# An order of 2,178 steps drawn anew, and a planner that lets each engine go on by itself: attention, SwiGLU and SoLU layers on one core

## The chip, the core and the metric

The kernel runs on one core of a Trainium2 chip. The metric is the device time of one execution in microseconds, as the median of several runs; less is better. The engines are named as in the profile: PE (TensorE, matmuls), DVE (VectorE), ACT (ScalarE), POOL (GpSimd) and SP (SyncE, which issues the DMAs).

## What is computed

```python
def _attn_ref(q, k, v):                      # q, k, v: (4, 8, 576, 64), float32
    scores = scale * np.matmul(q, k.transpose(0, 1, 3, 2))
    # heads 0-3: the last 32 keys; heads 4-7: every fourth of the last 128
    scores = np.where(masks[None], scores, -1000000000.0)
    scores = scores - np.max(scores, axis=-1, keepdims=True)
    attn = np.exp(scores)
    attn = attn / (np.sum(attn, axis=-1, keepdims=True) + 1e-09)
    return np.matmul(attn, v)
def _moe_ref(x, w_gate, w_val, w_out):       # x: (2304, 512), d_ff 1536
    g = x @ w_gate
    silu = g * (1.0 / (1.0 + np.exp(-g)))
    return silu * (x @ w_val) @ w_out
def _moe2_ref(x, w_in, w_out, g_ln):         # d_ff 1024
    h = x @ w_in
    e = np.exp(h - np.max(h, axis=-1, keepdims=True))
    solu = h * (e / (np.sum(e, axis=-1, keepdims=True) + 1e-09))
    # layer norm over d_ff, times g_ln
    return ln @ w_out
```

The weights are float64 in memory; each is turned into two float16 halves (a high part and the rest) on the chip, and so are the activations, so that three float16 products make one product of nearly float32's precision.

## The kernel before

**The work.** Attention is done by batch (4), pair of heads (4) and group of three blocks of 96 queries (2): 32 groups. A group runs scores on PE (line 1208), the maximum on DVE (L1230), exponentials with their sums on ACT (L1249), the inverse of the six sums per row on DVE (`inv`: L1262 adds 1e-9 and scales, L1264 is the reciprocal), the product with it on POOL (L1268), transposes on PE (L1293) and a copy of them to SBUF (L1301 on DVE, L1304 on ACT), the product with V (L1331), and the split of the output into two halves, on ACT (L600) and DVE (L605). Line 605 is a helper that writes the low half of any split, so tiles tell the uses apart: `x` is an attention output, `yhl` the output of the first MoE layer, `uhl` its hidden values, `area` and `gv` weights.

The 2,304 rows then go through the MoE layer in 12 chunks of 192 (`a_chunk`, six parts each, L1395: gate and value; `b_part`, L1479: the product with `w_out`), and through the second layer in 18 tiles of 128 (`c_part`, L1527; `d_part`, L1655). Thirteen slabs of weights are loaded by L669 in halves, converted on DVE, ACT and POOL (L685 to L741), given a scale common to the slab (L768, L793, L794 and a sum over partitions by PE, L544), and split. `w_rel`, called three times, makes the scales of several slabs relative to the largest of them: L894 to L896, and L901 in the second call.

**What sets the order.** Every piece of work is a *step*: an engine, a cost in microseconds, a function that issues its instructions, and the tiles it reads and writes. 2,178 steps are recorded; the table `PRI` gives each its place in one total order. `Plan.schedule` goes through that order once, with a model of times. The model decides two things: which PSUM bank a step gets, and how many *fillers* are put ahead of a PE step that has to wait. A filler is a matmul of ones (`idle`, L376) that nobody reads; it keeps PE active while it waits, and is issued only in the plan's first 320 us (`OPT["fill"]`). Each engine's queue is then the order restricted to that engine, and the queues run on the chip as their semaphores allow: a step whose inputs are late holds up what stands behind it on its engine.

In the model of before a step starts when its engine is free, its inputs are there and, for steps marked `port`, when no step of the other engine of DVE and POOL that is planned already overlaps it.

Of the kernel before, what the change touches and what calls it, by code (L numbers as in the profile page):

```python
# [1942 lines left out]
```

## Time and profile before

| | before |
|---|---|
| median of 3 runs | 753.19 us (752.01 to 753.53) |
| profiled execution | 754.8 us |
| its span, first to last instruction | 751.7 us |
| mean granted clock of PE | 0.986 of full speed |
| PE busy | 727.3 us (97%) |
| DVE busy | 503.2 us (67%) |
| ACT busy | 448.1 us (60%) |
| POOL busy | 236.5 us (31%) |
| fillers | 225, busy 31.4 us |

The shares are means over very different stretches. Up to about 200 us attention, the conversion of weights and the first chunks run side by side; from 280 us PE is busy without a gap. The busy time of PE holds the fillers, and matmuls that ran at the lower of PE's two clocks (the granted clock is the profile's column PEclk, 1.00 being full speed).

### The profile page before, as it was taken

The numbers are of one execution on the slowest core, as the hardware profiler recorded it, in microseconds if no ns is written. First come the engines' busy times: TensorE is split into PE (matmuls) and PEld (weight loads), VectorE is DVE, ScalarE is ACT, GpSimd is POOL, SyncE is SP. The second block draws the span as 40 slices with busy tenths as digits, with TensorE's granted clock in tenths as the row PEclk, the third lists the DMA queues.
The fourth block names the chain that finished last, engine by engine and source line by source line (L and its number), as shares of the span: only waits on it lengthen the run. The fifth ranks groups of instructions, "written<-read, shape, count | busy, mean of one in ns | idle before, by whom it ended". The sixth has DMA issues, their size and how long they took to land.

```text
span 751.7 us, 18305 instructions
## 1 busy us (share of the span) xinstructions
PE 727.3 (97%) x7488; PEld 601.0 (80%) x7488; DVE 503.2 (67%) x1059; ACT 448.1 (60%) x982; POOL 236.5 (31%) x188
## 2 busy tenths in 40 slices
PE   9868999999899999999999999999999999999998
PEld 7747989998897896678775989998776889968744
DVE  4989989899867877786787755366568222134562
ACT  5878997757566585976764664466554333334432
POOL 4525354865552331161252233314131000100000
PEclk9979999999999999999999999999999999999999
DMA  9797744236153614647455244213522100001021
GB/s 222 177 371 214 206 129 150 77 103 165 37 150 104 118 26 85 117 94 150 89 111 114 67 68 106 57 41 62 97 58 59 36 9 15 2 1 30 15 35 50
DMA packets 150195, 71.71 MB, mean 95 GB/s; under 512 B 136416, under 2 KB 136416, under 8 KB 149600
## 3 DMA queue, kind: packets, MB, share of 16 engines
q1 hardware_dynamic: 150112, 70.55, 39.0%
q8 instruction: 58, 0.95, 0.5%
q14 instruction: 25, 0.20, 0.1%
HBM read 46.14 MB, written 4.72 MB: 68 GB/s over the span
## 4 chain that ended last, share of the span: by engine, by line
PE 72%; DVE 7%; ACT 2%; issue 1%; POOL 0%; ACTq 0%; DVEq 0%; POOLq 0%
PE ps L1395 28%; PE ps L1479 16%; PE ps L1655 12%; PE ps L1527 12%; PE ps L1208 2%; PE ps L1336 1%; DVE area L715 1%; DVE uhl L605 1%; DVE uhl L596 0%; DVE wam L692 0%; PE ps L1331 0%; DVE sml L1230 0%; DVE area L605 0%; PE ps L1636 0%; DVE area L1561 0%
## 5 line engine op out<-in xcount | busy, mean ns | idle before, releaser
L1395 PE MATMUL ps<-x,gv 128*128 128x192 f16 x3456 | 296.1, 247 | 1.8 <-ACT ps L577 0.6
L1395 PEld LDWEIGHTS <-gv 128*128 128x128 f16 x3456 | 286.5, 98 | 7.3 <-issue 2.4
L1479 PE MATMUL ps<-uhl,area 128*128 128x192 f16 x1728 | 152.6, 247 | 1.6 <-DVE yhl L605 1.3
L1479 PEld LDWEIGHTS <-area 128*128 128x128 f16 x1728 | 143.7, 98 | 7.1 <-DVE yhl L605 1.5
L1527 PE MATMUL ps<-area,yhl 128*128 128x512 f16 x432 | 98.7, 379 | 0.0
L1655 PE MATMUL ps<-area 128*128 128x512 f16 x408 | 94.0, 379 | 0.0
L1268 POOL TENSOR_TENSOR sm<-sm,sml 96x768 f32<-96x768 f32 x28 | 45.5, 1627 | 126.3 <-DVE sml L1264 69.5
L1416 DVE SCALAR_TENSOR_TENSOR u<-ps,c_gv,si 128x384 f32<-128x384 f32 x60 | 36.5, 611 | 62.8 <-ACT si L1407 56.3
L1527 PEld LDWEIGHTS <-yhl 128*128 128x128 f16 x432 | 41.1, 98 | 46.0
L1407 ACT ACTIVATE si<-ps,c_gv 128x384 f32<-128x384 f32 x72 | 41.3, 578 | 53.6 <-PE ps L1395 49.1
L1655 PEld LDWEIGHTS <-area 128*128 128x128 f16 x408 | 38.8, 98 | 41.9 <-issue 0.2
L617 POOL TENSOR_TENSOR uhl<-u,uhl 128x768 f16<-128x768 f32 x12 | 20.1, 1686 | 92.3 <-ACT uhl L600 92.2
L685 POOL TENSOR_TENSOR area<-area 128x512 int32<-128x512 int32 x28 | 38.5, 1392 | 33.3 <-ACT area L698 11.0
L1587 POOL TENSOR_TENSOR sml<-sml,nhalf 128x2 f32<-128x2 f32 x18 | 12.9, 720 | 113.9 <-DVE sml L1584 113.9
L617 POOL TENSOR_TENSOR qk<-qk,qk 96x768 f16<-96x768 f32 x16 | 27.8, 1737 | 66.7 <-ACT qk L600 29.5
L1422 ACT ACTIVATE si<-u 128x384 f32<-128x384 f32 x60 | 31.0, 517 | 21.5 <-DVE u L1416 21.4
L1249 ACT ACTIVATE sm<-sm,sml 96x128 f32<-96x128 f32 x96 | 37.2, 388 | 6.1 <-DVE sml L1243 6.0
L1546 DVE TENSOR_REDUCE sml<-ps 128x1 f32<-128x1024 f32 x18 | 21.9, 1214 | 21.8 <-PE ps L1527 21.8
L1552 ACT ACTIVATE area<-ps,sml 128x1024 f32<-128x1024 f32 x18 | 21.7, 1203 | 22.1 <-DVE sml L1547 21.6
L605 DVE SCALAR_TENSOR_TENSOR area<-area,rel 128x512 f16<-128x512 f32 x30 | 26.2, 880 | 10.8 <-ACT area L600 10.7
L376 PE MATMUL ps<-ones 128*128 128x256 bf16 x225 | 31.4, 291 | 1.0 <-POOL ones L1681 1.0
L1607 ACT ACTIVATE area<-area,sml 128x1024 f32<-128x1024 f32 x17 | 20.9, 1238 | 18.5 <-DVE sml L1601 18.5
(226 smaller groups left out, 1131.0 us busy)
## 6 DMA issues: line engine op xcount, KB each, us to landing
area<-in_moe_w_out_dram SPq DMA_DIRECT2D x10, 1024.0 KB, 5.1
area<-in_moe_w_val_dram SPq DMA_DIRECT2D x6, 1024.0 KB, 7.7
area<-in_moe_w_gate_dram SPq DMA_DIRECT2D x6, 1024.0 KB, 9.9
out_dram<-area SPq DMA_DIRECT2D x18, 256.0 KB, 2.1
area<-in_moe_w_in_dram SPq DMA_DIRECT2D x4, 1024.0 KB, 5.1
qk<-in_v_dram SPq DMA_DIRECT2D x9, 384.0 KB, 4.0
v<-in_v_dram SPq DMA_DIRECT2D x49, 64.0 KB, 2.3
qk<-in_q_dram SPq DMA_DIRECT2D x20, 144.0 KB, 5.5
```

The source lines that it names most:

```text
L376: nc.tensor.matmul(out=to, lhsT=ones, rhs=ones.unsqueeze(1).to_broadcast([128, 2, 128]), start=True, stop=True)
L605: step("DVE", dve(n) + by + more, lambda: nc.vector.scalar_tensor_tensor(out=lo(), in0=src(), scalar=scale, in1=hi(), op0=ALU.mult, op1=AL ...
L617: step("POOL", n / 480 + 0.05, lambda: nc.gpsimd.tensor_tensor(out=lo(), in0=src(), in1=hi(), op=ALU.subtract), r=list(sk) + list(hk), w=lk)
L685: step("POOL", 1.23, lambda: nc.gpsimd.tensor_tensor(out=ti[:, x], in0=ti[:, x], in1=part[:, x], op=ALU.add), r=rk, w=tk)
L1249: nc.scalar.activation(out=smv[:, n], in_=view()[0:QB, n // 3, n % 3] if on_pe else smv[:, n], func=ACTF.Exp, bias=nm[:, n:n + 1], scale=c ...
L1268: step("DVE" if OPT["pn"][b] else "POOL", dve(768) if OPT["pn"][b] else 1.43, lambda: on.tensor_tensor(out=smv, in0=smv, in1=rs.unsqueeze( ...
L1395: nc.tensor.matmul(out=view()[:, ff, w], lhsT=wt[:, a, kk, (f % 4) * 128:(f % 4) * 128 + 128], rhs=x[:, c, kk, BLK * o:BLK * o + BLK], sta ...
L1407: step("ACT", act(384) + 0.06, lambda: nc.scalar.activation(out=si, in_=view()[:, :, 0], func=ACTF.Silu, scale=c_gv[:, b, 2 * ci:2 * ci + 1]),
L1416: nc.vector.scalar_tensor_tensor(out=uu, in0=view()[:, :, 1], scalar=c_gv[:, b, 2 * ci + 1:2 * ci + 2], in1=si, op0=ALU.mult, op1=ALU.mult)
L1479: nc.tensor.matmul(out=bk.get()[:, 0, cc * BLK:cc * BLK + BLK], lhsT=whl[6 + f // 4][:, a, f % 4, c * 128:(c + 1) * 128], rhs=uhl[:, e, f] ...
L1527: nc.tensor.matmul(out=bk.get()[:, half], lhsT=yhl[:, i, c, o:o + 128], rhs=w_in_hl[m][:, e, c % 2, half * 512:half * 512 + 512], start=(c ...
L1655: nc.tensor.matmul(out=bk.get()[:, 0], lhsT=zt[:, c, kk], rhs=whl[11 + half][:, e, kk % 4], start=(kk == 0 and n == 0), stop=(kk == 7 and ...
```

## The change

The table `PRI` is drawn anew. Its first steps of SP, 24 loads, come in the same order as before; behind these, steps of every engine change places. The planner no longer follows the total order: it takes from `PRI` a queue for each engine, and starts, again and again, the head of that queue which can start first. A step marked `port` waits only for a step of the other engine that already holds the port. Loads are planned with a limit on the rows in flight, and with corrections per load (`late`). Costs of several kinds of steps are changed a little. These numbers reach the chip only through the banks and the fillers: 248 instead of 225.

Two things change in what is computed with: the inverse of the sums of batches 0 and 1 (16 of the 32 groups), and `w_rel`, which now takes one column at a time.

```diff
+        queue = {e: [st for st in order if st["eng"] == e] for e in ("PE", "DVE", "ACT", "POOL", "SP")}
+        order = []
+
+        def head(eng):
+            if not queue[eng] or queue[eng][0]["left"]:
+                return no, False, None
+            st, opens = queue[eng][0], None
+            t = at = max(free.get(eng, 0.0), st["ready"])
             if st["port"]:
                 for a, b in held["POOL" if eng == "DVE" else "DVE"]:
-                    if a < t + cost and t < b:
+                    if a <= t < b:
                         t = b
+            held_up = t > at
...
+        while any(queue.values()):
+            heads = {eng: head(eng) for eng in queue}
+            eng = min(queue, key=lambda e: (heads[e][0], not heads[e][1]))
+            t, _, opens = heads[eng]
+            st = queue[eng].pop(0)
...
             nc.vector.reciprocal(out=m, in_=com[:, c:c + 1])
-            nc.vector.tensor_scalar(
-                out=rel[:, n0 - 6:n1 - 6], in0=wsc[:, 1, n0 + 2:n1 + 2], scalar1=m, scalar2=(1.0, 2.0 ** -16, 1024.0)[c],
-                op0=ALU.mult, op1=ALU.mult)
+            for n in range(n0 - 6, n1 - 6):
+                nc.vector.tensor_scalar(
+                    out=rel[:, n:n + 1], in0=wsc[:, 1, n + 8:n + 9], scalar1=m, scalar2=(1.0, 2.0 ** -16, 1024.0)[c],
+                    op0=ALU.mult, op1=ALU.mult)
...
         def inv():
+            if plain:
+                nc.vector.tensor_reduce(out=rs, in_=both, axis=AX.X, op=ALU.add)
+                nc.vector.reciprocal(out=rs, in_=rs)
+                return
             nc.vector.tensor_scalar(
                 out=su, in0=su, scalar1=1e-9, scalar2=1.0 if PV[b] == "f" else 2.0 ** -10, op0=ALU.add, op1=ALU.mult)
             nc.vector.reciprocal(out=rs, in_=su)
...
+        step("POOL", 0.1, lambda: nc.gpsimd.memset(sue, 1e-9), w=[("sue", n) for n in range(4)])
```

`both` is a tile of pairs: the exponentials' sums are accumulated into the first of each pair, and the second holds 1e-9. The table, of which every line differs, begins

```diff
-    32, 3, 2, 0, 15, 49, 4, 6, 5, 19, 76, 44, 126, 1, 22, 16, 85, 43, 93, 50, 46, 45, 108, 130,
+    18, 3, 5, 6, 2, 4, 47, 7, 8, 1, 13, 83, 45, 111, 0, 15, 11, 95, 44, 105, 64, 60, 51, 109,
```

Three places of the new order follow. Line numbers move by 33 to 61: L605 is L641 after, L692 L732, L768 L808, L704 L744, L710 L750, L894 to L901 are L936 to L945, L1262 and L1264 are L1305 and L1306, L669 is L709. The numbers behind the tiles' names count buffers.

On DVE, where the second `w_rel` is made (`rel`) and an attention output is split (`x1`, last row), before:

```order
L1262 TENSOR_SCALAR sml_111<-sml_111 96x6
L1264 RECIPROCAL sml_111<-sml_111 96x6
L710 TENSOR_SCALAR area_72<-area_72 128x1024
L1301 COPY et_102<-ps2_63 128x576
L559 TENSOR_SCALAR wsc_81<-ps4_65 128x1
L562 TENSOR_SCALAR wsc_81<-wsc_81 128x1
L565 RECIPROCAL wsc_81<-wsc_81 128x1
L894 TENSOR_REDUCE com_84<-wsc_81 128x1
L895 RECIPROCAL sml_111<-com_84 128x1
L896 TENSOR_SCALAR rel_85<-wsc_81,sml_111 128x2
L901 TENSOR_SCALAR rel_85<-rel_85 128x2
L605 SCALAR_TENSOR_TENSOR x1_104<-ps3_64,vsc_88,x1_104 128x288
```

and after:

```order
L892 SCALAR_TENSOR_TENSOR area_72<-area_72,wsc_82 128x1024
L732 TENSOR_REDUCE wam_81<-area_72 128x1
L641 SCALAR_TENSOR_TENSOR x1_105<-ps3_64,vsc_89,x1_105 128x288
L750 TENSOR_SCALAR area_72<-area_72 128x1024
L1305 TENSOR_REDUCE sml_112<-sue_79 96x6
L1306 RECIPROCAL sml_112<-sml_112 96x6
L744 TENSOR_SCALAR area_72<-area_72 128x1024
L1360 COPY et_103<-ps2_63 128x576
L808 TENSOR_SCALAR wam_81<-wam_81 128x1
L833 TENSOR_SCALAR wsc_82<-wam_81 128x1
```

The split (now L641 on `x1`) stands directly behind the reduction `wam`; the scale of the slab (L808, L833), the conversion (L750, L744), the copy to `et` and all of `w_rel`, which now begins five rows below these, come behind it.

On DVE, where the output of the first MoE layer is split (`yhl`), before:

```order
L1447 TENSOR_SCALAR sml_111<-rel_85,usc_87 128x1 x3
L583 TENSOR_REDUCE sml_111<-qk2_94 96x1
L605 SCALAR_TENSOR_TENSOR area_72<-area_72,glw_83 128x512
L605 SCALAR_TENSOR_TENSOR uhl_109<-u32_108,sml_111,uhl_109 128x768 x2
L605 SCALAR_TENSOR_TENSOR yhl_110<-ps3_64,rel_85,yhl_110 128x2x192
L1504 TENSOR_SCALAR sml_111<-usc_87,kh_86 64x1 x2
L605 SCALAR_TENSOR_TENSOR uhl_109<-u32_108,sml_111,uhl_109 128x768
```

and after:

```order
L1506 TENSOR_SCALAR sml_112<-rel_86,usc_88 128x1 x3
L641 SCALAR_TENSOR_TENSOR yhl_111<-ps3_64,rel_86,yhl_111 128x2x192
L641 SCALAR_TENSOR_TENSOR uhl_110<-u32_109,sml_112,uhl_110 128x768
L641 SCALAR_TENSOR_TENSOR area_72<-area_72,glw_84 128x512
L641 SCALAR_TENSOR_TENSOR uhl_110<-u32_109,sml_112,uhl_110 128x768 x2
L744 TENSOR_SCALAR area_72<-area_72 128x1024
L1606 TENSOR_REDUCE sml_112<-ps1_62 128x1
```

The split of `yhl` now stands ahead of the last split of `area` and of all three splits of `uhl`.

On SP, the loads of `w_val` (halves of slabs) after the loads of the second batch's q and k, before:

```order
L912 DMA qk1_93<-in_k_dram 96x6x64 x2
L669 DMA area_72<-in_moe_w_val_dram 128x4x256
L912 DMA qk0_92<-in_k_dram 96x6x64 x2
L669 DMA area_72<-in_moe_w_val_dram 128x4x256 x2
L912 DMA v32_1_91<-in_v_dram 96x2x64
L912 DMA v32_1_91<-in_v_dram 80x2x64
L912 DMA v32_1_91<-in_v_dram 48x2x64
L912 DMA v32_1_91<-in_v_dram 128x2x64
```

and after:

```order
L957 DMA qk1_94<-in_k_dram 96x6x64 x2
L709 DMA area_72<-in_moe_w_val_dram 128x4x256 x3
L957 DMA v32_0_91<-in_v_dram 96x2x64
L957 DMA v32_0_91<-in_v_dram 128x2x64 x5
L957 DMA qk0_93<-in_k_dram 96x6x64 x2
L957 DMA qk2_95<-in_k_dram 96x6x64 x2
L709 DMA area_72<-in_moe_w_out_dram 128x2x512 x2
L957 DMA gln_83<-in_moe2_g_ln_dram 128x8x1
```

Before, one half of `w_val` was issued, then a load of k, then two halves. Now three halves are issued in a row, and the half that came first comes third; k follows behind loads of v.

## Rows read from the trace of the kernel before

**Rows 1.** busy us (share of the span) and instructions of PE, from the page

```profile
PE 727.3 (97%) x7488; PEld 601.0 (80%) x7488; DVE 503.2 (67%) x1059; ACT 448.1 (60%) x982; POOL 236.5 (31%) x188
```

**Rows 2.** stretches; columns: us, busy and count by engine, PEclk, DMA share, GB/s

```profile
40.00:60.00 20.00, 11.08 (x109) 8.55 (x109) 18.01 (x36) 17.64 (x40) 7.36 (x6) 0.73 0.88 303
60.00:80.00 20.00, 19.22 (x217) 17.03 (x215) 19.04 (x35) 17.92 (x40) 6.50 (x5) 0.93 0.82 232
100.00:120.00 20.00, 18.11 (x203) 17.01 (x200) 16.44 (x32) 18.39 (x46) 13.47 (x10) 0.91 0.49 142
160.00:180.00 20.00, 18.99 (x238) 17.53 (x236) 17.63 (x43) 14.13 (x38) 13.35 (x10) 1.00 0.62 183
180.00:200.00 20.00, 17.47 (x197) 15.59 (x195) 19.22 (x35) 11.58 (x35) 11.19 (x8) 0.91 0.34 92
280.00:700.00 420.00, 420.00 (x4286) 338.24 (x4285) 244.78 (x536) 224.66 (x496) 97.44 (x74) 1.00 0.32 66
```

**Rows 3.** PE's timeline, 183 to 203 us; columns: start, us, engine, line, operation, operands

```profile
189.27 0.69 PE L1293 MATMUL ps<-ident,sm 96*128 96x96 f32 x6
...
195.10 0.72 PE L1331 MATMUL ps<-et,v 128*64 128x96 f32 x12 [2.17 <-DVE x L605]
195.75 1.04 PE L1293 MATMUL ps<-ident,sm 96*128 96x96 f32 x6
196.59 3.01 PE L1479 MATMUL ps<-uhl,area 128*128 128x192 f16 x18
...
200.22 1.65 PE L1479 MATMUL ps<-uhl,area 128*128 128x192 f16 x18
```

**Rows 4.** DVE's timeline, 186 to 203 us

```profile
189.94 0.65 DVE L710 TENSOR_SCALAR area<-area 128x1024 int32<-128x1024 int32 x1
...
191.36 0.15 DVE L562 TENSOR_SCALAR wsc<-wsc 128x1 f32<-128x1 f32 x1
...
191.99 2.43 DVE L896 TENSOR_SCALAR rel<-wsc,sml 128x2 f32<-128x2 f32 x1
...
194.54 0.51 DVE L605 SCALAR_TENSOR_TENSOR x<-ps,vsc,x 128x288 f16<-128x288 f32 x1
```

**Rows 5.** POOL's timeline, 188 to 196 us

```profile
190.19 1.73 POOL L1268 TENSOR_TENSOR sm<-sm,sml 96x768 f32<-96x768 f32 x1 [1.41 <-DVE sml L1264]
191.88 2.52 POOL L685 TENSOR_TENSOR area<-area 128x512 int32<-128x512 int32 x2
```

**Rows 6.** DVE's timeline, 254 to 266 us

```profile
258.36 0.46 DVE L1447 TENSOR_SCALAR sml<-rel,usc 128x1 f32<-128x1 f32 x3
...
262.11 0.61 DVE L605 SCALAR_TENSOR_TENSOR yhl<-ps,rel,yhl 128x384 f16<-128x384 f32 x1
```

**Rows 7.** PE's timeline at five other places

```profile
19.61 3.33 PE L376 MATMUL ps<-ones 128*128 128x256 bf16 x29
...
51.91 0.16 PE L544 MATMUL ps<-wsc,ones 128*128 128x1 bf16 x1 [3.81 <-DVE wsc L794]
...
58.91 0.24 PE L1395 MATMUL ps<-x,gv 128*128 128x192 f16 x1 [0.59 <-ACT ps L577]
...
177.00 0.72 PE L1331 MATMUL ps<-et,v 128*64 128x96 f32 x12 [0.77 <-DVE sml L1262]
...
262.77 3.39 PE L1479 MATMUL ps<-uhl,area 128*128 128x192 f16 x39 [1.26 <-DVE yhl L605]
```

**Rows 8.** DVE's timeline, 36 to 45 us

```profile
39.04 1.22 DVE L692 TENSOR_REDUCE wam<-area 128x1 f32<-128x1024 f32 x1 [1.59 <-DMA area<-in_moe_w_gate_dram]
```

**Rows 9.** SP's queue, 58 to 84 us

```profile
62.07 0.45 SPq L669 DMA_DIRECT2D area<-in_moe_w_val_dram  x1
...
68.61 0.98 SPq L669 DMA_DIRECT2D area<-in_moe_w_val_dram  x2
```

**Rows 10.** DMA issues of `w_val`, from the page: KB each, median us from issue to landing

```profile
area<-in_moe_w_val_dram SPq DMA_DIRECT2D x6, 1024.0 KB, 7.7
```

**Rows 11.** ScalarE's timeline, 76 to 82 us

```profile
78.39 1.14 ACT L718 ACTIVATE gv<-area 128x1024 f32<-128x1024 f32 x1
```

More of the change, by code (lines that the diff above doesn't have):

```diff
@@ L184, in __init__, with step @@
         self.steps, self.writer, self.readers, self.urgency = [], {}, {}, 0.0
-        self.lead, self.part = 0.0, ""
-    def step(self, eng, cost, fn, r=(), w=(), lat=0.0, tab=None, dense=1.0, starts=1, port=False):
+        self.lead, self.part, self.loads = 0.0, "", {}
+    def step(self, eng, cost, fn, r=(), w=(), lat=0.0, tab=None, dense=1.0, starts=1, port=False, rows=8, big=False, iss=0.54):
         deps = {}
-        for k in r:
+        for k in [*r, ("ones",)] if eng == "PE" else r:
             if k in self.writer:
@@ L199, in step @@
         st = {"n": len(self.steps), "eng": eng, "cost": cost, "fn": fn, "deps": list(deps.values()), "lat": lat,
-              "tab": tab, "dense": dense, "starts": starts, "port": port or eng == "POOL", "end": None, "left": len(deps), "outs": [], "part": self.part, "urg": self.urgency - self.lead, "ready": 0.0}
+              "tab": tab, "dense": dense, "rows": rows, "big": big, "iss": iss, "starts": starts, "port": port or eng == "POOL", "end": None, "left": len(deps), "outs": [], "part": self.part, "urg": self.urgency - self.lead, "ready": 0.0}
+        if eng == "SP":
+            n = self.loads[self.part] = self.loads.get(self.part, -1) + 1
+            late = OPT["late"].get(self.part, ())
+            st["lat"] += late[n] if n < len(late) else 0.0
         for d in st["deps"]:
@@ L237, in schedule @@
             order[at] = st
-        free, tab = {"SP": 1.9, "ACT": 1.9, "DVE": 0.6, "POOL": 0.6}, "exp"
+        free, tab = {"ACT": 1.9, "DVE": 0.6, "POOL": 0.6}, "exp"
         self.busy, self.warm, self.window = 0.0, False, 0
         no = float("inf")
-        bank_free, issued, done = [0.0] * 8, 0.6, []
+        bank_free = [0.0] * 8
+        sent, moved, was_big, loads = 0.0, 0.75, False, []
         held = {"DVE": [], "POOL": []}
@@ L291, in schedule @@
             if eng == "SP":
-                part, at = cost / max(st["starts"], 1), t
+                first = None
                 for _ in range(st["starts"]):
-                    issued = max(issued, st["ready"], done[-8] + 2.0 if len(done) >= 8 else 0.0) + 0.475
-                    at = max(at, issued - 0.475) + part
-                    done.append(at)
-                cost = at - t if st["starts"] else cost
+                    at = max(sent, st["ready"], loads[-8][1] + 2.3 if len(loads) >= 8 else 0.0)
+                    first = at if first is None else first
+                    sent, over = at + st["iss"], sum(x[2] for x in loads) + st["rows"] - 128
+                    for a, b, n in loads:
+                        if over <= 0:
+                            break
+                        if over <= n:
+                            sent = max(sent, a + over / n * (b - a))
+                        over -= n
+                    at = max(moved, at + 0.25)
+                    moved = at + cost / st["starts"] + (0.8 if st["big"] and not was_big else 0.0)
+                    loads.append((at, moved, st["rows"]))
+                    was_big = st["big"]
+                t, cost = first, moved - first
             st["start"], st["end"] = t, t + cost
-            free[eng] = t + cost
+            free[eng] = t + cost if eng != "SP" else sent
             if st["port"]:
-                held[eng] = held[eng][-7:] + [(t, t + cost)]
+                held[eng] = held[eng][-3:] + [(t, t + cost)]
             after = t + cost + self.PIPE[eng] + self.LAT
@@ L616, in split @@
         hi_on(way == 4, 1.0, True, act(n))
-        step("POOL", n / 480 + 0.05, lambda: nc.gpsimd.tensor_tensor(
-            out=lo(), in0=src(), in1=hi(), op=ALU.subtract), r=list(sk) + list(hk), w=lk)
+        for x in range(0, n, n // (OPT["pcs"][3] if flat else 1)):
+            x = slice(x, x + n // (OPT["pcs"][3] if flat else 1))
+            step("POOL", (x.stop - x.start) / 480 + 0.05, lambda x=x: nc.gpsimd.tensor_tensor(
+                **({"out": lo(), "in0": src(), "in1": hi()} if x.stop - x.start == n else
+                   {"out": lo()[:, x], "in0": src()[:, x], "in1": hi()[:, x]}), op=ALU.subtract),
+                r=list(sk) + list(hk), w=lk)
     place = [
@@ L912, in fn @@
                 nc.sync.dma_start(out=o, in_=i)
-        if not act:
-            step("SP", cost, fn, w=w, lat=DMA_LAT, starts=len(fns))
-            return
-        def fn_act():
-            for o, i in fns:
-                nc.scalar.dma_start(out=o, in_=i)
-        step("ACT", 0.45 * len(fns), fn_act, w=[w[0] + ("issue",)])
-        step("SP", cost, lambda: None, r=[w[0] + ("issue",)], w=w, lat=DMA_LAT, starts=0)
+        step("SP", cost, fn, w=w, lat=DMA_LAT, starts=len(fns), rows=rows, big=big)
     def loads(cost, fns, w, r=(), flip=False):
@@ L1171, in s1 @@
         smv = sm.rearrange("p j u t -> p (j u) t")
-        (nm, nk), (su, uk) = (small(12) for _ in range(2))
-        nm, su = nm[0:QB, 0:12:2], su[0:QB, 0:12:2]
+        nm, nk = small(12)
+        nm = nm[0:QB, 0:12:2]
+        plain = PV[b] != "d" and not LATE[b]
+        if plain:
+            both, uk = sue_ring.next()
+            su = both[:, :, 0]
+        else:
+            su, uk = small(12)
+            su = su[0:QB, 0:12:2]
         f32 = QK[b] == "f"
@@ L1455, in u_split @@
         t, tk = usl.pop(j)
+        first = len(P.steps)
         for n in range(3):
```

96 lines of the change are left out of this document (59 added, 37 removed), and 180 rows, old and new, of the table PRI.

## The prediction

> **What bounds the kernel now.** I read the busy table first, then the table by stretches, then PE's timeline at every idle gap of the bad stretches, and last the timelines of the engines that end those gaps. PE is busy 727.3 of 751.7 us [rows 1], so everything but its idle time and its slow clock is fixed work: the same real matmuls run after the change. The stretches tell where the rest lies [rows 2]. From 280 to 700 us PE is busy 420.00 of 420.00 at full clock: no order can give anything there, only take. The losses are ahead of it: 40 to 60 us (11.08 busy, clock 0.73), 60 to 80 (19.22, 0.93), 100 to 120 (18.11, 0.91), 160 to 180 (18.99) and 180 to 200 (17.47, 0.91). In those same stretches VectorE (DVE) is busy 16.44 to 19.22 of 20. The head is thus a chain through DVE, whose steps run in a fixed order; PE waits when the step it needs stands too far back in that order. That is what a new order can change.
>
> The clearest case is at 195 us. PE waits 2.17 us for the L605 split of an attention output [rows 3]. That split began at 194.54, and the two instructions ahead of it on DVE show why: L896, a TENSOR_SCALAR on two columns, took 2.43 us [rows 4], while GpSimd (POOL) ran a pair of L685 additions from 191.88 for 2.52 us [rows 5]. A one-column TENSOR_SCALAR, L562 at 191.36, took 0.15 us beside POOL's L1268, which ran from 190.19 for 1.73 us. After the wait PE's clock is at the lower of its two levels for a while: the six transposes of L1293 take 1.04 instead of 0.69, and 18 matmuls of L1479 take 3.01 instead of 1.65 [rows 3].
>
> **The change, term by term.** The sum is made against the profiled execution: 754.8 us, of which 751.7 are the span. It lies 1.6 us above the median of the runs, 753.19, so the result is moved down by that at the end.
>
> Term 1, the wait at 195 us. The split stands right behind the L692 reduction in the new DVE order; L768, L793, L794, both halves of the conversion L704 and L710, the L1301 copy and the whole of `w_rel` are now behind it. Their durations add up to 6.3 us, the stalled L896 among them, and its input, a matmul group, stands on PE far ahead of the wait. So the wait of 2.17 goes, and with it the slow clock behind it: (1.04 - 0.69) + (3.01 - 1.65) = 1.71. Together -3.9. What is late next is the split of the following output, which ends a PE chain of its own that moves forward as a whole. `w_rel` itself goes by single columns: two more instructions at 0.15, hidden, as the first split that reads its result stands nine DVE steps further back. Bounds: -1.5, if another DVE instruction ahead of a needed one is held as L896 was (2.43), and -4.4, if the three clock fillers behind it go too.
>
> The Trainium skill bears on this in "SBUF — State Buffer", section "Who interferes with whom": the second port pair of VectorE belongs to GpSimd as well, whoever starts first holds it for its whole instruction, and a tensor_scalar can be of the kind that needs it. The rows of L896 and L685 agree. The rule speaks against the change at one place: the new order puts the conversion L704 right behind the reciprocal that releases POOL's L1268; if POOL takes the pair first, L704 and the copy behind it, on which the next output depends, come up to 1.73 us later, and the total would be -4.6 instead of the -6.3 below. In the trace of before L710 stood at that place, began at 189.94 and took 0.65 though L1268 began at 190.19, so I don't count it.
>
> Term 2, the wait at 262.77 us. PE waits 1.26 for the split `yhl` [rows 7], which on DVE stood behind an L605 split of `area` and two of `u`, and began at 262.11 [rows 6]. Now it stands ahead of them, right behind the three L1447, which ended at 258.82. It can begin some 3 us earlier, over twice the wait, so all of the wait goes: -1.3, bounds -1.3 and 0.
>
> Term 3, up to the first MoE matmul at 58.91 [rows 7]. DVE idled 1.59 at 39.04 for a weight load [rows 8]; three steps that are ready are now put ahead of that reduction, and the splits of the first attention outputs come earlier. But PE's longest wait, 3.81 at 51.91 for a weight scale, grows rather than shrinks: its scale step has 1.8 us more DVE work ahead of it. Adding the durations of DVE's steps in either order up to the last split before the first MoE matmul gives 48.4 against 48.9 us, and part of the idle time is filled. I take -0.7. Bounds: -3 (the idle of 1.59 filled and half of the slow clock in 40 to 60 us gone) and +1 (the later scale not made up).
>
> Term 4, 60 to 120 us. PE is idle 0.78 in 60 to 80 and 1.89 in 100 to 120 [rows 2]. The order gives DVE steps that PE waits for 0.8 to 2 us less work ahead, but POOL and ScalarE, which end some of these waits, gain nothing. I take -1.0; bounds -2.7 (all idle time) and +2 (a wait as long as that at 195 us in a new place).
>
> Term 5, 160 to 180 us: idle 1.01, most of it one wait of 0.77 at 177.00 for DVE [rows 7]; the steps ahead of the one that ends it take about 2 us less in the new order. -0.7, bounds -1.0 and +0.5.
>
> Term 6, fillers. 248 instead of 225 clock fillers are issued, 21 of the 23 before the first MoE matmul. One takes 3.33 / 29 = 0.115 us [rows 7], together 2.6. Behind a wait they are free; where the data come sooner than the plan thought, they are paid. I take half, +1.3, bounds 0 and 2.6.
>
> The new form of the sum's inverse: 16 times a TENSOR_SCALAR of 96x6 becomes a TENSOR_REDUCE of 96x12 that reads pairs. The trace of before has no such reduction. Its price lies between nothing and the 1.22 us of the 128x1024 reduction [rows 8]; with 12 columns I put it at the 0.15 of the smallest DVE instruction, which is about what it replaces, so nothing. The constant that the pairs read is set once by POOL at the start, while PE runs fillers only.
>
> From 280 us on the orders differ by single steps, and PE never waits there: 0. The tail is the same: 0.
>
> Sum: -3.9 - 1.3 - 0.7 - 1.0 - 0.7 + 1.3 = -6.3. 754.8 - 6.3 = 748.5, and 1.6 lower on the scale of the median: **747 us**.
>
> **Rivals.** *A, no gain.* DVE is near full in the whole head, so a step moved forward moves another back, and PE then waits for that one. For it: 19.22 of 20 busy in 180 to 200 us. Against it: the wait there was made by a 2.43 us stall, not by work. Then term 1 shrinks to -1.5, terms 3 to 5 give nothing and the fillers cost all of 2.6: -1.5 - 1.3 + 2.6 = -0.2, 753.0 us. That also is the case in which the plan's picture of the chip doesn't hold and the order does not do what it says.
>
> *B, slower.* SP issues loads in order and waits at each. Half of `w_val` (the L669 issued at 62.07 [rows 9]) stands in the new order behind two other halves, which in before were issued at 68.61, once a DVE step had freed their place. It is then issued at about 69.6 and lands, by the median of 7.7 us [rows 10], at 77.3. ScalarE's L718 needs it at 78.39 [rows 11], 1.1 us of room, and DVE's next conversion stands behind that. If it lands later, ScalarE and then DVE stop with all that is queued behind, and each us goes on to the path, since DVE is the chain there. It decides the sign from a landing 1.1 + 6.3 + 1.5 = 8.9 us beyond 77.3; at 11 us late, 9.9 are lost: -6.3 + 9.9 = +3.6, 757 us. For it: 1.1 us is little. Against it: the landing would have to take twice the median.
>
> *C, a larger gain.* All idle time of terms 3 and 4 goes and no filler is paid: -3.9 - 1.3 - 3.0 - 2.7 - 1.0 = -11.9, 741.3 us. For it: the plan now puts each engine's steps where their inputs are ready. Against it: several of these waits are for POOL, ScalarE or a load.
>
> **Chances and range.** The forecast, 744.5 to 750.5 us, has 0.60; A (751 to 755) 0.15; B 0.11; C 0.14. A measurement of this kernel can tell about 0.2%, 1.5 us, from no change. Faster by more: the forecast, C and a fifth of A, 0.77. Within: most of A and a little of B, 0.10. Slower: 0.13. The range 741 to 753.5 leaves out B, half of C and the upper part of A, about 0.2.
>
> **What would show it.** In the profile after: no PE wait near 191 to 196 us and a clock of 1.00 in that stretch (term 1); no wait for the `yhl` split near 256 us (term 2); the first MoE matmul about 58 us (term 3); 100 to 120 us with less than 1.9 idle (term 4); waits behind the fillers no shorter than before (term 6). Each column of `w_rel` near 0.15 us. The forecast is wrong if the first MoE matmul starts after 60 us, if ScalarE waits for `w_val` near 78 us, or if PE shows any idle time between 280 and 700 us.

## The result, and the profile after

| | before | after |
|---|---|---|
| median, 8 runs each | 753.36 us | 746.49 us (744.71 to 750.58) |
| ratio, 95% interval | | 0.9918 (0.9894 to 0.9942) |
| profiled execution, span | 754.8, 751.7 us | 746.4, 744.4 us |
| fillers | 225, 31.4 us | 248, 35.1 us |

The changed kernel is faster, by 6.9 us at the median; 747.0 was forecast. The ratio is worked out over the fast runs alone, without one run of the kernel before that took 1499.92 us, and is not the quotient of the two medians; by it the gain is 6.2 us. The busy table and the stretches of the changed kernel (the columns are those of [rows 1, 2]):

```profile
PE 724.8 (97%) x7511; PEld 599.8 (81%) x7511; DVE 500.8 (67%) x1064; ACT 446.1 (60%) x980; POOL 233.2 (31%) x189
```

```profile
40.00:60.00 20.00, 15.00 (x149) 11.98 (x147) 19.07 (x33) 18.94 (x45) 9.74 (x10) 0.87 1.09 354
60.00:80.00 20.00, 19.12 (x220) 16.89 (x218) 18.17 (x33) 18.53 (x38) 5.14 (x4) 0.96 0.99 286
100.00:120.00 20.00, 17.07 (x202) 16.08 (x201) 18.62 (x28) 17.86 (x45) 11.14 (x9) 1.00 0.33 111
160.00:180.00 20.00, 19.95 (x257) 18.16 (x255) 18.56 (x40) 15.06 (x49) 14.68 (x11) 1.00 0.59 193
180.00:200.00 20.00, 19.25 (x240) 18.48 (x239) 18.43 (x42) 13.08 (x28) 11.97 (x9) 1.00 0.30 71
280.00:700.00 420.00, 418.70 (x4291) 339.06 (x4290) 240.53 (x538) 219.60 (x485) 95.58 (x72) 1.00 0.32 65
```

Against [rows 2], the stretches 160 to 200 us are nearly full and at full clock. From 100 to 120 us PE is idle longer than before, 2.93 against 1.89 us, though its clock no longer falls; and from 280 us on there are 1.30 us of idle time where there were none.

Where the time went can be read from one curve. For each profile the durations of PE's matmuls, fillers left out and each counted as it lasts at full clock, are summed from the start; the lag is how much later a kernel has done what the kernel before had done by a given time (negative: it is ahead). In us, at the times of the kernel before:

| profile | 60 | 80 | 120 | 160 | 185 | 205 | 260 | 263 | 400 | 420 | 740 |
|---|---|---|---|---|---|---|---|---|---|---|---|
| after | -1.25 | -1.59 | -1.23 | -1.42 | -3.10 | -6.92 | -6.92 | -8.35 | -8.33 | -7.08 | -7.35 |
| e2_inverse (order of before) | +0.80 | +1.91 | +1.65 | +1.57 | +1.55 | +1.50 | +1.50 | +1.48 | +1.47 | +1.47 | +1.47 |
| e1_columns | -0.87 | -0.87 | -1.40 | -1.62 | -1.63 | -4.41 | -4.41 | -4.38 | -4.38 | -4.38 | -4.39 |
| e3_split_first | -0.48 | -0.47 | -1.50 | -1.43 | -1.44 | -3.27 | -3.27 | -3.27 | -3.27 | -3.27 | -3.27 |
| e6_pair_of_columns | -0.69 | -1.30 | -0.94 | -1.06 | -2.74 | -5.95 | -5.95 | -7.38 | -7.35 | -6.70 | -6.66 |
| e8_split_last | -2.40 | -2.46 | -2.20 | -2.39 | -4.07 | -5.40 | -5.40 | -6.83 | -6.81 | -6.15 | -6.43 |
| e9_split_and_eviction | -1.71 | -1.63 | -3.33 | -2.97 | -4.64 | -8.46 | -8.46 | -9.89 | -9.87 | -9.27 | -9.54 |

The second line, of a kernel that differs from the one before by 16 small instructions, shows how far one execution can stray in the first 80 us: 1.9. Behind that the curves of kernels with one order run flat together, so steps there of more than a few tenths are put down to the kernel. The changed kernel gains at three places: 160 to 185 (-1.7), 185 to 205 (-3.8) and 262 us (-1.4), and loses 1.2 at 410. The steps at 160 to 185 and at 262 us come out alike in the three other profiles of the new order in the table (experiments 6, 8 and 9). The profiled executions differ by another 1.1 us outside the span (754.8 - 751.7 = 3.1 before, 746.4 - 744.4 = 2.0 after), but this is the one execution and not the change: over the 57 executions of the kernel before that were timed with the experiments the time outside the span has a median of 1.8 us, over the eight of the changed kernel one of 2.0.

**The place of term 1.** PE, DVE and POOL of the changed kernel; the columns are start, duration, engine, line, operation:

```profile
188.79 0.72 PE L1390 MATMUL ps<-et,v 128*64 128x96 f32 x12
189.44 0.71 PE L1352 MATMUL ps<-ident,sm 96*128 96x96 f32 x6
189.99 1.65 PE L1539 MATMUL ps<-uhl,area 128*128 128x192 f16 x18
191.57 0.72 PE L1390 MATMUL ps<-et,v 128*64 128x96 f32 x12
```

```profile
184.37 1.21 DVE L732 TENSOR_REDUCE wam<-area 128x1 f32<-128x1024 f32 x1
185.50 0.50 DVE L641 SCALAR_TENSOR_TENSOR x<-ps,vsc,x 128x288 f16<-128x288 f32 x1
...
189.73 0.33 DVE L939 TENSOR_SCALAR rel<-wsc,sml 128x1 f32<-128x1 f32 x2
189.98 0.27 DVE L945 TENSOR_SCALAR rel<-rel 128x1 f32<-128x1 f32 x2
```

```profile
188.76 2.54 POOL L725 TENSOR_TENSOR area<-area 128x512 int32<-128x512 int32 x2
```

The split begins at 185.50, right behind the reduction, and the product with V that waited for it, now at 188.79, waits for nothing (the one at 191.57 is the next product, at 199.53 in [rows 3]): the 2.17 of [rows 3] are gone, the transposes take 0.71 instead of 1.04 and the 18 matmuls 1.65 instead of 3.01. The columns of `w_rel` pass beside POOL's pair of additions, 0.33 and 0.27 for two each, where the two-column form took 2.43 [rows 4, 5].

**The place of term 2,** on DVE and then on PE:

```profile
247.73 0.75 DVE L641 SCALAR_TENSOR_TENSOR area<-area,glw 128x512 f16<-128x512 f32 x1
...
249.97 0.45 DVE L1506 TENSOR_SCALAR sml<-rel,usc 128x1 f32<-128x1 f32 x3
250.34 0.61 DVE L641 SCALAR_TENSOR_TENSOR yhl<-ps,rel,yhl 128x384 f16<-128x384 f32 x1
```

```profile
254.43 6.10 PE L1539 MATMUL ps<-uhl,area 128*128 128x192 f16 x72
```

The split of `yhl` follows the scales at once, and the matmuls that waited 1.26 in [rows 7] begin without a wait, four us behind it.

**PE's waits that are left,** of over 0.8 us from 57 us on:

```profile
58.21 1.99 PE L1454 MATMUL ps<-x,gv 128*128 128x192 f16 x12 [1.56 <-DVE x L641]
...
63.32 0.71 PE L1352 MATMUL ps<-ident,sm 96*128 96x96 f32 x6 [0.88 <-POOL sm L1326]
...
110.64 0.71 PE L1141 MATMUL ps<-ident,qk 96*128 96x96 f32 x6 [1.90 <-ACT sm L1291]
...
410.17 1.07 PE L1454 MATMUL ps<-x,gv 128*128 128x192 f16 x11 [1.23 <-ACT area L1728]
```

The last two are new; so is a shorter one, 0.75 at 186.60, for ScalarE's L613. Behind the first of them stands a split, on DVE, and the four POOL instructions that it lies beside:

```profile
101.81 4.50 DVE L641 SCALAR_TENSOR_TENSOR gv<-area,wsc,gv 128x1024 f16<-128x1024 f32 x1
106.24 1.21 DVE L732 TENSOR_REDUCE wam<-area 128x1 f32<-128x1024 f32 x1
107.37 0.94 DVE L1272 TENSOR_REDUCE sml<-ps 96x6 f32<-96x768 f32 x1
```

```profile
100.47 2.27 POOL L912 TENSOR_TENSOR gv<-gv,gv 128x512 f16<-128x512 f32 x2
102.70 2.53 POOL L725 TENSOR_TENSOR area<-area 128x512 int32<-128x512 int32 x2
```

```profile
108.41 0.36 ACT L1291 ACTIVATE sm<-ps,sml 96x128 f32<-96x128 f32 x1 [1.91 <-DVE sml L1305]
```

The same split took 1.27 in the kernel before, at 107.66. Here it ends at 106.31, 1.08 behind the end of POOL's last instruction. The row maximum L1272 behind it ends at 108.31, ScalarE's exponentials begin 0.10 later, the last of six ends at 110.59, and PE goes on at 110.64. This is the wait that term 4's upper bound names, and it is the order's: it is 1.90 in experiment 6 and 1.89 in experiment 8 too.

The second new wait starts with an eviction on ScalarE:

```profile
409.44 0.69 ACT L1728 ACTIVATE area<-ps,sml 128x512 f32<-128x512 f32 x1 [1.60 <-DVE x L641]
```

PE had its own inputs with the split that ended at 409.35 and waited 0.8 more, until the eviction ended at 410.13, for the bank that it frees. In the program the eviction waits for that same split, so it can't begin before 409.35. Experiments 6, 8 and 11 leave this place as it is; there PE comes to it after the split and waits 0.63, 0.63 and 0.64, for the eviction alone.

**Loads.** SP issues the three halves of `w_val` in a row, with no wait for a place, and ScalarE's L758 is not late (it stood at 78.39 in [rows 11]; this execution is some 1.5 us ahead there):

```profile
61.90 1.55 SPq L709 DMA_DIRECT2D area<-in_moe_w_val_dram  x3
```

```profile
76.93 1.14 ACT L758 ACTIVATE gv<-area 128x1024 f32<-128x1024 f32 x1
```

### The profile page after: what moved, and what is told of

It is laid out like the page before. It is cut to its first block, busy times and chain, and to the rows that moved or that the text cites. A ratio compares the mean times of both kernels' runs of the same rounds, so it can differ in the third digit from the quotient of the medians.

```text
span 744.4 us, 18369 instructions
## 1 busy us (share of the span) xinstructions
PE 724.8 (97%) x7511; PEld 599.8 (81%) x7511; DVE 500.8 (67%) x1064; ACT 446.1 (60%) x980; POOL 233.2 (31%) x189
## 4 chain that ended last, share of the span: by engine, by line
PE 85%; DVE 4%; SPq 3%; POOL 2%; DMA 2%; ACT 2%; issue 2%; ACTq 0%; POOLq 0%
PE ps L1454 37%; PE ps L1539 18%; PE ps L1715 12%; PE ps L1587 11%; SPq L957 3%; PE ps L1250 2%; DMA qk<-in_q_dram 1%; PE ps L1395 1%; PE ps L1390 1%; PE ps L1352 1%; DMA out_dram<-area 1%; POOL sm L1326 1%; POOL area L725 1%; PE ps L410 0%; POOL area L912 0%
## 5 line engine op out<-in xcount | busy, mean ns | idle before, releaser
L1539 PE MATMUL ps<-uhl,area 128*128 128x192 f16 x1728 | 150.7, 246 | 0.1
L1326 POOL TENSOR_TENSOR sm<-sm,sml 96x768 f32<-96x768 f32 x28 | 42.5, 1519 | 112.7 <-DVE sml L1310 28.1
L641 DVE SCALAR_TENSOR_TENSOR area<-area,rel 128x512 f16<-128x512 f32 x30 | 26.6, 893 | 19.7 <-ACT area L636 19.6
L410 PE MATMUL ps<-ones 128*128 128x256 bf16 x248 | 35.1, 295 | 4.6 <-ACT ps L613 2.9
L410 PEld LDWEIGHTS <-ones 128*128 128x128 bf16 x248 | 25.5, 106 | 9.4 <-issue 3.0
L1621 DVE SCALAR_TENSOR_TENSOR area<-ps,sml,area 128x1024 f32<-128x1024 f32 x18 | 23.0, 1278 | 13.9 <-ACT area L1612 13.9
```

What stands on the lines that cost most here:

```text
L410: nc.tensor.matmul(out=to, lhsT=ones, rhs=ones.unsqueeze(1).to_broadcast([128, 2, 128]), start=True, stop=True)
L1326: step("POOL", 0.1 + 1.33 * size / 6, lambda x=x: nc.gpsimd.tensor_tensor(out=smv[:, x], in0=smv[:, x], in1=rs[:, x].unsqueeze(2).to_broad ...
L1539: nc.tensor.matmul(out=bk.get()[:, 0, cc * BLK:cc * BLK + BLK], lhsT=whl[6 + f // 4][:, a, f % 4, c * 128:(c + 1) * 128], rhs=uhl[:, e, f] ...
```

## Experiments

Every ratio is against the kernel before; lines and tiles are named as in the profiles. A step's move is shown on its engine, since in the table it is a shift of numbers.

**1. `w_rel` by columns, in the order of before.**

```diff
-    nc.vector.tensor_scalar(out=rel[:, n0 - 6:n1 - 6], in0=wsc[:, 1, n0 + 2:n1 + 2], ...
+    for n in range(n0 - 6, n1 - 6):
+        nc.vector.tensor_scalar(out=rel[:, n:n + 1], in0=wsc[:, 1, n + 8:n + 9], ...
```

> The kernel before with w_rel by single columns and nothing else. Theory 1 (the wait at 195 us comes from one stalled instruction, L896, two columns wide, beside POOL's additions): the columns take about 0.2 us each, DVE reaches the split some 2 us earlier, the PE wait of 2.17 and the slow clock behind it go, -3 to -4 us, although the split keeps its place in the order. Rival (the place in the order is what counts, and POOL's hold moves to the next DVE instruction): the wait stays above 1.5 us and the time is the same, within 1 us.

749.6 us, ratio 0.9966 (0.9954 to 0.9978). Its DVE at the place:

```profile
190.36 0.33 DVE L897 TENSOR_SCALAR rel<-wsc,sml 128x1 f32<-128x1 f32 x2
190.61 0.27 DVE L903 TENSOR_SCALAR rel<-rel 128x1 f32<-128x1 f32 x2
190.80 0.51 DVE L605 SCALAR_TENSOR_TENSOR x<-ps,vsc,x 128x288 f16<-128x288 f32 x1
```

The split begins at 190.80 instead of the 194.54 of [rows 4] without having been moved (this execution was 1.6 ahead by then), and 2.8 us are gained between 185 and 205. The stall, not the order, made most of that wait.

**2. The new inverse alone,** in the order of before.

```diff
+                nc.vector.tensor_reduce(out=rs, in_=both, axis=AX.X, op=ALU.add)
+                nc.vector.reciprocal(out=rs, in_=rs)
```

> The kernel before with the inverse of the sums as a reduction over pairs (16 groups) and nothing else. Theory: 0.15 us for the reduction instead of 0.17 to 0.41 for the TENSOR_SCALAR, which can also be held by POOL; in all -1 to 0 us. Rival (the new form is a good part of the whole gain, since it frees DVE from POOL in 16 places): -2 us or more.

752.47 us, ratio 1.0003 (0.9993 to 1.0013): nothing. In the changed kernel the 16 reductions have this line of the table by form:

```profile
L1305 DVE TENSOR_REDUCE sml<-sue 96x6 f32<-96x12 f32 x16 | 2.4, 151 | 0.0
```

**3. Only the split of term 1 moved,** in the kernel before.

```diff
 L692 TENSOR_REDUCE wam<-area 128x1
+L605 SCALAR_TENSOR_TENSOR x_104<-ps_64,vsc,x_104 128x288
 L768 TENSOR_SCALAR wam<-wam 128x1
...
 L901 TENSOR_SCALAR rel<-rel 128x2
-L605 SCALAR_TENSOR_TENSOR x_104<-ps_64,vsc,x_104 128x288
```

> The kernel before with one DVE step moved: the split of the attention output goes from behind w_rel to directly behind the reduction L692, as in the changed kernel; w_rel keeps its two-column form. Theory 2 (term 1 of the prediction): the wait of 2.17 and the slow clock go, -3.9 us (-1.5 to -4.4). Rival (DVE is full, what is moved back is waited for instead): PE waits for the copy L1301 or a scale instead, 0 to -1 us.

750.82 us, ratio 0.9983 (0.9972 to 0.9994). DVE, then PE:

```profile
186.98 0.50 DVE L605 SCALAR_TENSOR_TENSOR x<-ps,vsc,x 128x288 f16<-128x288 f32 x1
...
190.85 2.45 DVE L896 TENSOR_SCALAR rel<-wsc,sml 128x2 f32<-128x2 f32 x1
...
195.39 0.85 DVE L605 SCALAR_TENSOR_TENSOR x<-ps,vsc,x 128x288 f16<-128x288 f32 x1
```

```profile
196.30 0.16 PE L544 MATMUL ps<-sml,ones 128*128 128x1 bf16 x1 [1.08 <-DVE sml L979]
```

The wait for this split goes, but `w_rel` is still held for 2.45 us, and now the instructions behind it are late: PE waits 1.08 for L979. Some 1.8 of the 3.8 us are gained.

**4. Only the split of `yhl` moved,** in the kernel before.

```diff
 L1447 TENSOR_SCALAR sml<-rel,usc 128x1 x3
+L605 SCALAR_TENSOR_TENSOR yhl<-ps_64,rel,yhl 128x2x192
 L583 TENSOR_REDUCE sml<-qk_94 96x1
 L605 SCALAR_TENSOR_TENSOR area<-area,glw 128x512
 L605 SCALAR_TENSOR_TENSOR uhl<-u_108,sml,uhl 128x768 x2
-L605 SCALAR_TENSOR_TENSOR yhl<-ps_64,rel,yhl 128x2x192
```

> The kernel before with one other DVE step moved: the split of yhl at 262 us goes ahead of the reduction L583 and the splits of area and u, right behind L1447. Theory (term 2): the wait of 1.26 us goes and nothing else changes, -1.3 us. Rival (the splits of u that stand behind it are needed next, so the wait only moves): 0.

751.9 us, ratio 0.9999 (0.9988 to 1.001). DVE, then PE:

```profile
256.22 2.06 DVE L605 SCALAR_TENSOR_TENSOR area<-area,glw 128x512 f16<-128x512 f32 x1
...
259.44 0.61 DVE L605 SCALAR_TENSOR_TENSOR yhl<-ps,rel,yhl 128x384 f16<-128x384 f32 x1
259.96 0.94 DVE L583 TENSOR_REDUCE sml<-qk 96x1 f32<-96x768 f32 x1
...
261.49 1.94 DVE L605 SCALAR_TENSOR_TENSOR uhl<-u,sml,uhl 128x768 f16<-128x768 f32 x2
```

```profile
263.47 2.72 PE L1479 MATMUL ps<-uhl,area 128*128 128x192 f16 x31 [1.17 <-DVE uhl L605]
```

The plan's limit for fillers is lowered from 320 to 225 us with it, so that none is added: their number and places, all banks and all other queues are as before. The split ran early, as asked, and the wait stayed: the matmuls read `uhl` too, and its splits now end last. The wait had only been named after `yhl`.

**5. The new planner, columns and inverse, in the order of before** (262 fillers). The table holds the old order, with the one new step put in:

```diff
-    18, 3, 5, 6, 2, 4, 47, 7, 8, 1, 13, 83, 45, 111, 0, 15, 11, 95, 44, 105, 64, 60, 51, 109,
+    33, 3, 2, 0, 16, 4, 50, 5, 7, 6, 20, 77, 45, 127, 1, 23, 17, 86, 44, 94, 51, 47, 46, 109,
```

> The changed kernel with the order of before: the new planner with its costs (it sets banks and fillers alone), w_rel by columns and the new inverse. Theory (the order and the columns make the gain, the planner nothing): the time of the kernel before with columns, 0.995 to 0.998 of before, 749 to 751 us. Rival (the new planner's fillers and banks make a good part of it): below 748 us, or above 753 if its fillers cost.

750.68 us, ratio 0.9969 (0.9955 to 0.9983), the same as the columns alone. The planner's new model, with the banks and fillers that follow from it, buys nothing in the old order; the rest of the gain comes with the new order.

**6. The changed kernel with the two-column `w_rel` of before** (the edit of experiment 1 taken back).

```diff
-    for n in range(n0 - 6, n1 - 6):
-        nc.vector.tensor_scalar(out=rel[:, n:n + 1], ...
+    nc.vector.tensor_scalar(out=rel[:, n0 - 6:n1 - 6], ...
```

> The changed kernel with the two-column form of w_rel (L896, L901 of before) and nothing else changed. Theory (a two-column TENSOR_SCALAR is held while POOL runs its pair of additions, and in the new order the splits behind it are held with it, as in the run with the split moved alone): one more stall of 2.2 us on DVE near 190 us, PE waits for the next split or scale, +1 to +2 us against the changed kernel, 747.5 to 748.5. Rival (the new order alone is enough there): the same as the changed kernel within 0.7 us.

746.62 us, ratio 0.9928 (0.9904 to 0.9953): not distinguishable from the changed kernel. DVE, and POOL beside it:

```profile
190.09 0.42 DVE L938 TENSOR_SCALAR rel<-wsc,sml 128x2 f32<-128x2 f32 x1
190.54 1.15 DVE L943 TENSOR_SCALAR rel<-rel 128x2 f32<-128x2 f32 x1
```

```profile
189.12 2.54 POOL L725 TENSOR_TENSOR area<-area 128x512 int32<-128x512 int32 x2
```

The pair is still held, 0.42 and 1.15, but in this order POOL's additions are further on when it comes, and the split that PE waits for is ahead of it. In the curve 3.2 us are gained from 185 to 205 instead of 3.8. Order and columns thus mostly stand in for each other.

**7. The changed kernel, the 4.50 us split put behind two reductions.**

```diff
-L641 SCALAR_TENSOR_TENSOR gv_70<-area,wsc,gv_70 128x4x256
 L732 TENSOR_REDUCE wam<-area 128x1
 L1272 TENSOR_REDUCE sml<-ps_62 96x6
+L641 SCALAR_TENSOR_TENSOR gv_70<-area,wsc,gv_70 128x4x256
```

> The changed kernel with one DVE step moved: the split of a weight half (L641 on gv) that took 4.50 us at 101.8 goes behind two reductions that read one input (L732, L1272). Theory (it was held by three POOL instructions in a row, 100.5 to 105.2 us, and the exponentials behind the second reduction, on which PE waits 1.90 at 110.6, were late by that): the split takes 1.3 to 2.5 us, the wait goes, -1.5 to -2 us against the changed kernel, 744.5 to 745. Rival (another DVE instruction is held in its place, or the wait is for ScalarE's own work): 746 to 747, no difference.

745.56 us (742.69 to 749.73), ratio 0.9908 (0.9879 to 0.9938): by the times not distinguishable from the changed kernel. In its profile the wait at 110 is gone, and the split, now later in POOL's run, takes less; but this execution lost some 3 us between 60 and 80 us, in front of POOL's L1326, where executions stray. DVE, then PE:

```profile
106.49 2.53 DVE L641 SCALAR_TENSOR_TENSOR gv<-area,wsc,gv 128x1024 f16<-128x1024 f32 x1
```

```profile
62.74 0.71 PE L1352 MATMUL ps<-ident,sm 96*128 96x96 f32 x6 [2.54 <-POOL sm L1326]
```

**8. The changed kernel, the split of term 1 put back behind `w_rel`,** with no fillers ahead of the step that waits for it.

```diff
-            if st.get("fill"):
+            if st.get("fill") and st["part"] != "z130":
...
 L732 TENSOR_REDUCE wam<-area 128x1
-L641 SCALAR_TENSOR_TENSOR x_105<-ps_64,vsc,x_105 128x288
 L750 TENSOR_SCALAR area<-area 128x1024
...
 L945 TENSOR_SCALAR rel<-rel 128x1 x2
+L641 SCALAR_TENSOR_TENSOR x_105<-ps_64,vsc,x_105 128x288
```

> The changed kernel with the split of the attention output moved back behind w_rel, as in the order of before (w_rel by columns; no fillers ahead of the step that waits for it). Theory (with columns nothing is stalled there, as the kernel before with columns showed no wait at that place): 0 to +0.7 us against the changed kernel, 746.5 to 747.2. Rival (the place in the order is worth the 3.9 us of term 1 by itself): 749.5 to 750.5.

747.87 us, ratio 0.9939 (0.9917 to 0.9961). In the profile 1.3 us are gained from 185 to 205 instead of 3.8. Of the 2.5 that lack, 2.1 are these 18 fillers, which the changed kernel hasn't and which the plan put ahead of the following transposes:

```profile
188.86 2.14 PE L410 MATMUL ps<-ones 128*128 128x256 bf16 x18
```

What the old place of the split itself costs with columns that aren't held is not shown: the plan, taking the split to be late, also gave the product with V that waited for it another bank, so that product begins at 188.21, ahead of the split at 189.21. What is shown is that a plan which takes a split to be late can pay for it in fillers.

**9. Two steps of the changed kernel moved:** the split as in experiment 7, and the eviction for which PE waited at 410 us.

```diff
 L1612 ACTIVATE area,sml<-ps_63,sml 128x1024
+L1728 ACTIVATE area<-ps_62,sml 128x512
 L636 ACTIVATE vhl<-v_0_91 128x768
-L1728 ACTIVATE area<-ps_62,sml 128x512
```

> The changed kernel with two steps moved: on DVE the gv split that took 4.50 us at 101.81 stands behind L732 and L1272, and on ScalarE the eviction L1728, for which PE waited 1.23 us at 410.17, stands ahead of the L636 that ended at 407.84. Theory (the chain of DVE and the order at these two places made the waits): the wait of 1.90 at 110.64 and that at 410.17 both go, 746.5 - 1.9 - 1.2 = 743.4 us, and the difference to the changed kernel in the profile stands at 110 and at 410 us and nowhere else. Rival (a wait only moves on to what DVE does next, as it did for the yhl split): 746 to 747, with a new wait between 111 and 120 us or behind 410 us.

743.45 us (742.67 to 744.21), ratio 0.9870 (0.9852 to 0.9888): faster than the changed kernel, their intervals don't overlap. PE, ScalarE and PE:

```profile
108.55 0.71 PE L1141 MATMUL ps<-ident,qk 96*128 96x96 f32 x6
```

```profile
402.32 0.69 ACT L1728 ACTIVATE area<-ps,sml 128x512 f32<-128x512 f32 x1 [0.74 <-PE ps L1715]
```

```profile
407.98 3.21 PE L1454 MATMUL ps<-x,gv 128*128 128x192 f16 x37 [0.57 <-DVE x L641]
```

The wait at 110 is gone. At 410 a wait of 0.57 for the split stays; what the eviction added to it goes. The plan also gives these matmuls another bank than the eviction's, and other banks to 1,628 of the matmuls from 405 us on, so the earlier eviction and the other bank are not told apart. Nor are the two moves in the time; by the curve the first gives more, since the loss at 410 us is 0.6 here and 0.7 in experiments 6 and 8.

**10. The same with 29 instead of 13 fillers at 60 us.**

```diff
+            if st["eng"] == "PE" and st["part"] == "y010" and st.get("fill"):
+                st["fill"] += 16
```

> The two moves of the run before, and 29 instead of 13 clock fillers ahead of the transposes that waited for POOL's L1326 at 62.74 us in one profile and at 63.32 in another. Theory (the time that executions of the changed kernel lose between 60 and 75 us hangs on the clock falling there): the granted clock of 60 to 80 us is 1.00 instead of 0.9, the wait at 62 to 63 us is filled, and the median is 1 to 2 us below the run before. Rival (the fillers are paid, POOL is not late): 16 x 0.115 = 1.8 us more than the run before.

742.79 us (742.65 to 743.8), ratio 0.9867 (0.9852 to 0.9883), the lowest median of all; from experiment 9 it can't be told apart. Its stretch has no idle time and full clock (0.98 in experiment 9):

```profile
60.00:80.00 20.00, 20.00 (x246) 18.49 (x244) 18.14 (x34) 18.61 (x37) 3.98 (x4) 1.00 0.99 298
```

**11. The changed kernel with half the fillers in each place behind 45 us** (208 of 248).

```diff
-                self.idle(st["fill"], st["spare"])
+                self.idle(st["fill"] if st["end"] < 45.0 else st["fill"] // 2, st["spare"])
```

> The changed kernel with half the clock fillers in each place behind 45 us (40 fewer of 248; nothing else moves). Theory of term 6 (half of the fillers' time is paid): 40 x 0.115 / 2 = 2.3 us faster, 744.2. Rival (they stand in waits that last anyway and keep the clock up): the clock falls to the lower level behind the waits near 60, 111 and 188 us, and the time is 2 to 5 us longer, 748.5 to 751.5.

746.47 us (744.44 to 747.55), ratio 0.9910 (0.9894 to 0.9926): not distinguishable from the changed kernel. Neither theory holds; the clock does fall,

```profile
60.00:80.00 20.00, 18.23 (x177) 16.03 (x176) 16.25 (x29) 16.63 (x35) 5.62 (x5) 0.75 0.97 255
...
100.00:120.00 20.00, 17.64 (x196) 16.39 (x194) 18.52 (x32) 18.01 (x47) 12.52 (x9) 0.91 0.36 127
```

to 0.75 and 0.91 (0.96 and 1.00 in the changed kernel), and by the curve this execution is 3.0 us behind the changed kernel's at 120 us; at 740 us it is 1.2 behind (-6.19 against -7.35). That what fewer fillers save and what the lower clock costs cancel in the medians is a guess: this execution, 747.55 us, is the slowest of the six, and others stray by as much in the first 80 us.

## Why the prediction was right, and where not

| term | forecast, us | measured (curve of lags) |
|---|---|---|
| 1, wait at 195 | -3.9 | -3.8 (185 to 205) |
| 2, `yhl` at 262 | -1.3 | -1.4 |
| 3, up to the first MoE matmul | -0.7 | -0.7 at that matmul (58.91 to 58.21), -1.25 at 60, fillers included |
| 4, 60 to 120 | -1.0 | 0.0 |
| 5, 160 to 180 | -0.7 | -1.7 (160 to 185) |
| 6, fillers | +1.3 | not seen apart; most lies in term 3's place |
| from 280 on | 0 | +1.0, of it +1.2 at 410 |

The measured steps, with -0.2 between 120 and 160, add up to -7.3; with the 1.1 outside the span that is the 8.4 between the two profiled executions, against a forecast of 6.3. The execution of the kernel before that was profiled lay 1.6 us above the median, which the prediction takes off, and the 1.1 are part of these. The forecast of the median was 0.5 us too high. Behind 160 us the curve gives -5.9, nearly all of the 6.2 that the ratio gives; what lies ahead of 160 us is within what executions stray.

*Term 1* was right in size and place, but its reason was half the reason. It was put down to the order. Experiment 1 shows that ending the stall alone gives 2.8, experiment 3 that the new place alone gives 1.8, and experiment 6 that the whole new order without the columns gives 3.2. The two halves overlap, since either keeps PE from waiting for one DVE instruction that POOL holds. (The 6.3 us of steps put behind the split count also the inverse of the sums, 0.36, and L559 to L565, 0.45, which the text doesn't name; the term doesn't change by it.) The prediction used the Trainium skill here ("SBUF — State Buffer", "Who interferes with whom") and feared that L704 and the copy would be held behind POOL's L1268. They were not: L744 took 0.65 at 186.82, before POOL began at 187.07.

*Term 2* has the right number for a wrong step: "It can begin some 3 us earlier, over twice the wait, so all of the wait goes". Experiment 4 made it begin 2.7 us earlier and gained nothing. What the changed order did besides was to put the reduction L583 (0.94) ahead, one split of `uhl` in front of that of `area`, and the whole group at a moment when POOL holds nothing: the split of `area` and `glw` takes 0.75 where it took 2.06 beside POOL in experiment 4. Which of the three ends the wait, no run shows, so the number came right by luck.

*Term 3* fits in size, but part of that is luck. 21 of the 23 fillers more stand ahead of the first MoE matmul, so the -0.7 there is to be held against -0.7 and most of term 6's +1.3 together, that is, against a small loss. And one execution shows little: over the profiles that matmul begins between 58.38 and 60.05 in the order of before (experiments 1 to 5 and the kernel before) and between 56.98 and 58.69 in the new one (experiments 6 to 11 and the changed kernel). The new order is thus ahead there by about 1 us, more than forecast, although the weight scale does come later, as forecast (its matmul at 52.66 instead of 51.91); no run shows by which of its steps.

*Term 4* failed. Its step was "The order gives DVE steps that PE waits for 0.8 to 2 us less work ahead": it counted work ahead by undisturbed durations, and the new order put a split with two inputs in SBUF beside four POOL instructions in a row (4.50 instead of 1.27). Waits for POOL and ScalarE of 0.89 and 0.64, at 102.55 and 103.90 in the kernel before, went, and this one came. Experiment 9 takes it out, and 60 to 120 us then gives -1.6. The stray of 1.9 in the first 80 us is as large as the term, so only the wait itself, not the term's remainder, is shown.

*Term 5* was too small by 1.0. PE now idles 0.05 instead of 1.01 from 160 to 180 us, which is the most that the term allowed; 0.4 more come between 180 and 185, outside its stretch. No run took it apart.

*Term 6* took half of the fillers' time to be paid. With 40 fillers fewer the time is the same (experiment 11), and a median 2.3 lower was expected; so those 40 are no cost that can be seen. Single ones are: the 18 of experiment 8.

*From 280 on* the prediction said 0 and named idle time there as a sign that the forecast is wrong. That sign came, 1.30 us, of it 1.23 in the wait at 410. The step that failed is "the orders differ by single steps". In the two programs 157 of the 595 DVE instructions and 79 of ScalarE's 335 behind 280 us are out of the old sequence, and at one place the plan gave the MoE matmuls a bank that a late eviction still held.

That the median came within 0.5 us is luck in part: what terms 3, 5 and 6 gave beyond the forecast is about what term 4 and the wait at 410 took.

Of the rivals, A's mechanism (a step moved forward moves another back) decided term 4 but not the sum; B did not start, since no half of `w_val` waited for a place and ScalarE's instruction was as far ahead as the whole execution. C did not come: 741.3 is below every run on record, and only a further change comes near it, experiment 10 with the waits at 60 and 110 us mended and the eviction moved.

## What to carry to other kernels

When DVE and POOL share a stretch, look first for DVE instructions that take several times their usual time; a wait of PE behind one is ended by another form (single columns), by another place, or by a reduction put in the slot, and each of these alone may be enough. A wait is named after the input that came last: before moving that one, list all inputs of the waiting instruction and when each would be there. A new total order makes new waits as well as it ends old ones; reading the waits that are left in its profile, and moving two steps, gave 3 us more.
